# U W1's eight products kept together on TensorE, landmark sums on GpSimd, Newton's first batch ahead of the first weights

## The chip, the core and the metric

The kernel runs on one core of one Trainium2 chip. The metric is the device time of one launch in microseconds. The core has five engines that run side by side, each through its own queue in order: TensorE (matrix products; PE in the rows, its weight loads PEld), VectorE (DVE), ScalarE (ACT), GpSimd (POOL) and SyncE (SP), which here issues the loads.

## What is computed

A Nyström attention with 32 landmarks, then two gated layers of experts without routing. Batch 4, 8 heads, 576 positions, head size 64, so 2304 rows of 512; the hidden size of both layers is 1536. Everything is float32.

```python
q_lm = q.reshape(B, H, m, S // m, D).mean(axis=3)      # m = 32
k_lm = k.reshape(B, H, m, S // m, D).mean(axis=3)
A, Bm, C = sm(q, k_lm), sm(q_lm, k_lm), sm(q_lm, k)    # softmax of scaled products
Z = Bm.T / (norm1(Bm) * norminf(Bm) + 1e-06)
for _ in range(6):
    Z = 2 * Z - Z @ Bm @ Z
x = (A @ Z @ C @ v), rows (b, s), columns (h, d)
x = (silu(x @ w_gate) * (x @ w_val)) @ w_out           # layer 1
x = (sigmoid(x @ w2_gate) * (x @ w2_val)) @ w2_out     # layer 2
```

## The kernel before

The attention's output is never formed. With U = Z C v (32 x 64 per head), layer 1's input product is A (U W1), so the kernel forms U W1 and multiplies it with A. The work is cut into words of a list, each with a batch b, a half g of the heads (four each) or a chunk c of 256 hidden columns:

- F (`front`, lines 111 to 211), for (b, g): the landmark sums of keys and queries (`lm_steps`, `lm`, lines 118 to 122: VectorE adds 18 rows into one, ScalarE copies the result into the second half), their transposition by TensorE (`lt`, line 125), transposition of keys and queries (`tp`), the landmark scores (`cs`, `bm`), exponentials, their transposition (`et`), the products with v (`cv`, scaled into `bc` at line 193), and A's scores (`as`).
- B (`back`, line 231), for b: norms, then Newton's six steps for both halves (`nw` on TensorE, `rw` on VectorE, lines 262 to 284) and the transposition into `UT`. A's normalisation (`a_steps`, line 213) is stepped between Newton's steps.
- U (`uw_steps`, line 413), for (c, b): two PSUM tiles `pu`, one per half, each filled by four products of 64 rows, 32 weight columns and 512 moving columns. Four heads lie in four column strips and the two halves in two row strips of the array, so the eight products use eight different parts of it. Each is two matmul rows in a trace, as the operands are full float32. Afterwards a sum of high and low parts (`split`) goes to SBUF as `uw`.
- G (`gv1_steps`, `pg`, `pv`) and O (`o1_steps`, `po`), for (c, b): the gate and value products with A, and the product with the output weights, 48 matmul rows each.
- I and J: step the weights of a chunk until its input part (four quarters h of `W1`) or its output part is ready. A weight piece is loaded by SP into one of three `raw` buffers and converted by two ScalarE and two VectorE instructions (`convert`, lines 303 to 326), for output weights a split follows.

The order of words up to chunk 1 is written out by hand (line 575); words joined by + are stepped alternately. From chunk 2 on a loop takes U, O of the batch before, and G. Layer 2 follows.

Within that, the tile framework orders each engine's queue: it keeps program order as priority and lets an instruction that is ready by its own estimate go ahead of earlier ones that are not. The order is fixed when the program is built; on the chip each queue is followed strictly. Buffers of a tag (`bufs`) are reused in turn. PSUM tag "o" (two buffers) holds `cs` and `as` of batch 0 and, for c below `OA` = 2, the U and O tiles; from c = 2 on U and O tiles alternate between "o" and "a" (two buffers each). The values `vin` have one buffer, the keys and queries (`in`) four.

Of the kernel before, what the change touches and what calls it, by code (L numbers as in the profile page):

```python
# [9 lines left out]
ALU = mybir.AluOpType  # L10
AX = mybir.AxisListType
# [3 lines left out]
def nystrom_moe_kernel(tc, q, k, v, wg1, wv1, wo1, wg2, wv2, wo2, out):  # L15
    nc = tc.nc
    B, H, S, D = q.shape
    M = 32
    P = 128
# [23 lines left out]
    def ptile(shape, tag, name):  # L43
        return psum.tile(shape, F32, tag=tag, name=name, bufs=PB[tag])
# [4 lines left out]
    ident = cst.tile([P, P], F32, tag="ident", name="ident")  # L49
# [6 lines left out]
    UT = [cst.tile([P, 4, M], F32, tag=f"ut{b}", name=f"ut{b}") for b in range(B)]  # L56
# [4 lines left out]
    def mm(o, l, r, start=True, stop=True):  # L61
        nc.tensor.matmul(o, l, r, start=start, stop=stop, skip_group_check=True)  # L62
# [15 lines left out]
    NU = L // 2  # L78
# [3 lines left out]
    def flat(x):  # L82
        return x.rearrange("p a b -> p (a b)")

    def load_next(b, g, which):
        i = AORDER.index((b, g)) + (1 if which == "v" else 2)
        if i < len(AORDER):
            load_attn(AORDER[i][0], which, AORDER[i][1])
# [12 lines left out]
    def small(tag, shape, nm_, bufs=2):  # L101
        return att.tile(shape, F32, tag=tag, name=f"{tag}{nm_}", bufs=bufs)

    def pst(b, shape, nm, g=0):

        tag = "n" if nm in ("nw", "ut") else "a"
        if b == 0:
            tag = {"tp": "gv", "cs": "o", "as": "o"}.get(nm, tag)
        return ptile(shape, tag, f"{nm}_{b}_{g}")

    def front(b, g):

        nm_ = f"{b}_{g}"

        def sm(tag, shape, bufs=2):
            return small(tag, shape, nm_, bufs)

        def lm_steps(which):
            src = inq[which, b, g]
            lm = sm("lm", [P, 2, D])  # L120
            nc.vector.tensor_reduce(lm[:, 0], src.rearrange("p u d -> p d u"), axis=AX.X, op=ALU.add)  # L121
            nc.scalar.copy(lm[:, 1], lm[:, 0])
            yield
            ps = pst(b, [P, P], "lt", g)
            nc.tensor.transpose(ps, flat(lm), ident)
            bdt = sm("bd" + which, [P, 2, P], 1)
            for w in range(2):
                nc.scalar.activation(bdt[:, w], ps, AF.Copy, scale=pmask[:, w:w + 1])
            yield
            t = sm("kq", [P, NU, P])  # L130
            for i in range(3):
                ps = pst(b, [P, 3, P], "tp", g)
                for j in range(3):
                    u = 3 * i + j
                    nc.tensor.transpose(ps[:, j], flat(src[:, 2 * u:2 * u + 2]), ident)  # L135
                nc.scalar.copy(t[:, 3 * i:3 * i + 3], ps)
                yield
            load_next(b, g, which)
            return bdt, t

        bdk, kT = yield from lm_steps("k")
        bdq, qT = yield from lm_steps("q")
        if g == 0:
            BS[b] = (small("bs", [P, 2, M], b), small("bsm", [P, 2], b), small("bc", [P, 2, 96], b))
        bs, bsm, BC = BS[b]

        cmx = sm("cmx", [P, 2])
        csm = sm("csm", [P, 2])
        nmx = sm("nmx", [P, 1])
        e = sm("e", [P, 3, 2, M, 3], 1)  # L150
        pcs = []
        for w in range(2):
            ps = pst(b, [P, NU, M], "cs", g)
            for h in range(4):
                hs = slice(M * h, M * h + M)
                mm(ps[hs], bdq[:, w, hs], kT[:, :, hs])
            nc.vector.tensor_reduce(cmx[:, w:w + 1], flat(ps), axis=AX.X, op=ALU.max)
            pcs.append(ps)
            yield
        nc.vector.tensor_scalar(nmx, cmx[:, 0:1], cmx[:, 1:2], -1.0, op0=ALU.max, op1=ALU.mult)  # L160
        for w in range(2):
            nc.scalar.activation(e[:, :, w].rearrange("p r t j -> p j r t"),  # L162
                                 pcs[w].rearrange("p (j r) t -> p j r t", r=3), AF.Exp,
                                 bias=nmx, scale=1.0, accum_out=csm[:, w:w + 1])
        yield

        bmx = sm("bmx", [P, 1])
        ps = pst(b, [P, M], "bm", g)
        for h in range(4):
            hs = slice(M * h, M * h + M)  # L170
            mm(ps[hs], bdq[:, 0, hs], bdk[:, 0, hs])
        nc.vector.tensor_reduce(bmx, ps, axis=AX.X, op=ALU.max)
        nc.vector.tensor_scalar(bs[:, g], ps, bmx, None, op0=ALU.subtract)
        nc.scalar.activation(bs[:, g], bs[:, g], AF.Exp, scale=8.0, accum_out=bsm[:, g:g + 1])

        rc = sm("rc", [P, 1])
        nc.vector.tensor_scalar(rc, csm[:, 0:1], csm[:, 1:2], 1e-9, op0=ALU.add, op1=ALU.add)
        nc.vector.reciprocal(rc, rc)
        yield
        eT = sm("eT", [TP, R, P], 1)  # L180
        for hf in range(2):
            ps = pst(b, [TP, 3, P], "et", g)
            for j in range(3):
                r = 3 * hf + j
                nc.tensor.transpose(ps[:, j, :], flat(e[:, r // 2, r % 2]), ident)  # L185
            nc.scalar.copy(eT[:, 3 * hf:3 * hf + 3, :], ps)
            yield
        ps = pst(b, [P, D], "cv", g)
        for r in range(R):
            for h in range(4):  # L190
                mm(ps[32 * h:32 * h + 32, :], eT[:, r, 32 * h:32 * h + 32],
                   inq["v", b, g][:, h, r, :], start=(r == 0), stop=(r == R - 1))
        nc.vector.tensor_scalar(BC[:, g, M:M + D], ps, rc, None, op0=ALU.mult)
        load_next(b, g, "v")
        yield

        s = SX[b, g] = sm("sx", [P, L, M], 3)
        amx = sm("amx", [P, L])
        for i0, i1 in ((0, 5), (5, NU)):
            ps = pst(b, [P, 5, 2 * M], "as", g)  # L200
            for i in range(i0, i1):
                for h in range(4):
                    hs = slice(M * h, M * h + M)
                    mm(ps[hs, i - i0].rearrange("p (w m) -> p w m", w=2), qT[:, i, hs], bdk[:, :, hs])
            x = flat(ps[:, 0:i1 - i0]).rearrange("p (u m) -> p u m", m=M)
            us = slice(2 * i0, 2 * i1)
            nc.vector.tensor_reduce(amx[:, us], x, axis=AX.X, op=ALU.max)
            nc.vector.tensor_tensor(s[:, us], x, amx[:, us, None].to_broadcast([P, 2 * (i1 - i0), M]),
                                    op=ALU.subtract)
            nc.scalar.activation(s[:, us], s[:, us], AF.Exp)  # L210
            yield
# [19 lines left out]
    def back(b):  # L231

        def sm(tag, shape, bufs=2):
            return small(tag, shape, b, bufs)
# [34 lines left out]

        ga = [a_steps(b, g) for g in range(2)]  # L270
        ps = prod(BC)
        RW = sm("rw", [P, 2, 96], 3)
        nc.vector.tensor_tensor(RW, ps, rr[:, :, None].to_broadcast([P, 2, 96]), op=ALU.mult)
        yield
        for it in range(5):
            ps = prod(RW)
            RW2 = sm("rw", [P, 2, 96], 3)
            nc.vector.scalar_tensor_tensor(RW2, RW, 2.0, ps, op0=ALU.mult, op1=ALU.subtract)
            RW = RW2
            step(ga)  # L280
            yield
        ps = prod(RW)
        UU = flat(sm("rw", [P, 2, 96], 3))[:, 0:P].rearrange("p (g d) -> p g d", g=2)
        nc.vector.scalar_tensor_tensor(UU, RW[:, :, M:], 2.0, ps[:, :, M:], op0=ALU.mult, op1=ALU.subtract)
        yield
        ps = pst(b, [P, P], "ut")
        nc.tensor.transpose(ps, flat(UU), ident)
        nc.vector.tensor_copy(flat(UT[b]), ps)
# [10 lines left out]
    W1 = {}  # L299
# [92 lines left out]
    OA = 2  # L392
# [17 lines left out]
    def uw_steps(c, b):  # L410
        pss = [ptile([P, 2 * FC], otag(0, c), f"pu{c}_{b}_{g}") for g in range(2)]

        for g in range(2):
            rows = slice(D * g, D * g + D)
            for h in range(4):
                mm(pss[g][M * h:M * h + M, :], UT[b][rows, h, :], W1[c][rows, h].rearrange("p a b -> p (a b)"))
        for g in range(2):
            w = p1r.tile([P, 2, 2 * FC], F32R, tag="uw", name=f"uw{c}_{b}_{g}", bufs=3)
            UW[c, b, g] = w
            split(w[:, 0, :], w[:, 1, :], pss[g])  # L420
            yield
# [140 lines left out]
    def emit(word, nw=1):  # L562
# [10 lines left out]

    wfill.extend(weights(0, c) for c in range(2))
    first = (
        "I0+F00 F01 B0+F10 U00 F11 J0 B1 G00 I1 F20 U10 J1 O00 G10 O10 U01 G01 F21 U11 "
        "B2+F30 O01 G11 F31 U02 O11 G02 B3 U12 O02 G12 U03 O12 G03 U13 O03 G13"
    )
    for w in first.split():
        emit(w)  # L580
# [77 lines left out]
```

## Time and profile before

| | us |
|---|---|
| median of three runs | 918.42 (917.91 to 919.18) |
| profiled execution | 917.74 |
| its span, first to last instruction | 915.9 |
| TensorE busy in it | 877.8 |
| VectorE busy | 542.2 |
| ScalarE busy | 391.7 |
| GpSimd busy | 0.7 |

A busy TensorE is not TensorE at its peak: matmuls overlap in its pipeline, and a matmul alone counts its whole passage. Two levels of its clock occur: a granted clock of 1.00 is 2.4 GHz, 0.50 is 1.2 GHz, and a value between is a mean over a stretch. The timeline, the table by stretch and the chain of waits (followed back from the end, each step to what released it) are the other views used.

### The profile page before, as it was taken

The numbers are of one execution on the slowest core, as the hardware profiler recorded it, in microseconds if no ns is written. First come the engines' busy times: TensorE is split into PE (matmuls) and PEld (weight loads), VectorE is DVE, ScalarE is ACT, GpSimd is POOL, SyncE is SP. The second block draws the span as 40 slices with busy tenths as digits, with TensorE's granted clock in tenths as the row PEclk, the third lists the DMA queues.
The fourth block names the chain that finished last, engine by engine and source line by source line (L and its number), as shares of the span: only waits on it lengthen the run. The fifth ranks groups of instructions, "written<-read, shape, count | busy, mean of one in ns | idle before, by whom it ended". The sixth has DMA issues, their size and how long they took to land.

```text
span 915.9 us, 16047 instructions
## 1 busy us (share of the span) xinstructions
PE 877.8 (96%) x6588; PEld 741.9 (81%) x6588; DVE 542.2 (59%) x1093; ACT 391.7 (43%) x853; POOL 0.7 (0%) x6
## 2 busy tenths in 40 slices
PE   5499899999999999999999999999999999999997
PEld 4356877778898998998998888888888888888886
DVE  6988857746968678769961154346238236323343
ACT  5568568545725446428652263134116114111111
POOL 0000000000000000000000000000000000000000
PEclk9599999999999999999999999999999999999999
DMA  7666211003513113203110022003004000000132
GB/s 230 222 209 182 70 53 49 7 1 93 155 31 93 47 47 116 69 1 95 46 44 4 0 71 68 1 28 110 0 1 138 1 1 24 1 0 1 47 93 69
DMA packets 27081, 57.66 MB, mean 63 GB/s; under 512 B 4224, under 2 KB 7296, under 8 KB 27008
## 3 DMA queue, kind: packets, MB, share of 16 engines
q1 hardware_dynamic: 25280, 54.28, 19.6%
q10 hardware_dynamic: 1728, 2.36, 1.1%
q8 instruction: 51, 0.84, 0.4%
q14 instruction: 22, 0.18, 0.1%
HBM read 51.90 MB, written 4.72 MB: 62 GB/s over the span
## 4 chain that ended last, share of the span: by engine, by line
PE 88%; DVE 5%; ACT 4%; DMA 1%; issue 1%; SPq 0%; ACTq 0%
PE po L62 33%; PE pg L62 24%; PE pv L62 23%; PE pu L62 3%; PE tp L135 2%; PE nw L62 1%; DMA qin<-in_q_dram 1%; DVE lm L121 1%; PE cs L62 1%; ACT e L162 1%; PE as L62 1%; DVE hl L351 0%; ACT L162 0%; PE et L185 0%; DVE h L441 0%
## 5 line engine op out<-in xcount | busy, mean ns | idle before, releaser
L62 PE MATMUL po<-hh,wo 128*128 128x288 f32 x768 | 162.1, 302 | 1.1 <-DVE uw L351 0.7
L512 DVE TENSOR_TENSOR hf<-hf,pv 128x512 f32<-128x512 f32 (+1 forms) x60 | 38.0, 634 | 193.0 <-PE pv L62 193.0
L62 PE MATMUL po<-wo,h 128*128 128x512 f32 x648 | 152.2, 390 | 0.0
L62 PEld LDWEIGHTS po<-wo,h 128*128 128x128 f32 x648 | 121.1, 188 | 25.4 <-ACT h L350 0.3
L62 PEld LDWEIGHTS po<-hh,wo 128*128 128x128 f32 x768 | 123.0, 188 | 21.1 <-issue 14.4
L62 PE MATMUL pg<-AH,w 128*128 128x512 f32 (+1 forms) x480 | 136.1, 368 | 0.0
L62 PE MATMUL pv<-AH,w 128*128 128x512 f32 (+1 forms) x480 | 136.0, 368 | 0.0
L62 PE MATMUL po<-hl,wo 128*128 128x288 f32 x384 | 114.8, 299 | 0.3 <-DVE hl L351 0.3
L511 ACT ACTIVATE hf<-pg 128x512 f32<-128x512 f32 (+1 forms) x60 | 33.2, 554 | 165.4 <-PE pg L62 158.3
L62 PE MATMUL pg<-AH,uw 128*128 128x288 f32 x576 | 98.7, 298 | 2.3 <-ACT uw L350 1.8
L62 PEld LDWEIGHTS pg<-AH,w 128*128 128x128 f32 x480 | 87.3, 188 | 15.4
L62 PEld LDWEIGHTS pv<-AH,w 128*128 128x128 f32 x480 | 87.1, 189 | 15.0
L62 PE MATMUL pv<-AH,uw 128*128 128x288 f32 x576 | 96.7, 296 | 1.2 <-ACT sg L439 1.2
L62 PEld LDWEIGHTS pg<-AH,uw 128*128 128x128 f32 x576 | 83.1, 188 | 8.4 <-ACT uw L350 4.9
L350 ACT CAST h<-hf 128x512 fp32r<-128x512 f32 (+1 forms) x60 | 34.6, 576 | 123.2 <-DVE hf L512 123.2
L533 DVE TENSOR_TENSOR oacc<-po,oacc 128x512 f32<-128x512 f32 x90 | 61.9, 691 | 41.1 <-PE po L62 39.9
L62 PEld LDWEIGHTS pv<-AH,uw 128*128 128x128 f32 x576 | 82.9, 188 | 3.2 <-ACT sg L439 2.2
L62 PE MATMUL pg<-x1l,w 128*128 128x512 f32 x192 | 74.7, 389 | 0.0
L62 PE MATMUL pv<-x1l,w 128*128 128x512 f32 x192 | 74.7, 389 | 0.0
L62 PEld LDWEIGHTS po<-hl,wo 128*128 128x128 f32 x384 | 72.3, 188 | 2.4 <-issue 0.9
L467 DVE TENSOR_TENSOR acc<-po,acc 128x288 f32<-128x288 f32 x128 | 56.0, 452 | 18.2 <-PE po L62 17.5
L439 ACT ACTIVATE sg<-pg 128x288 f32<-128x288 f32 x96 | 39.2, 409 | 51.7 <-PE pg L62 51.1
(113 smaller groups left out, 1062.8 us busy)
## 6 DMA issues: line engine op xcount, KB each, us to landing
raw<-in_moe_w_out_dram SPq DMA_DIRECT2D x24, 512.0 KB, 4.2
raw<-in_moe_w_gate_dram SPq DMA_DIRECT2D x48, 128.0 KB, 3.3
raw<-in_moe_w_val_dram SPq DMA_DIRECT2D x48, 128.0 KB, 3.1
raw<-in_moe_w_gate_dram SPq DMA_DIRECT2D x24, 256.0 KB, 2.9
raw<-in_moe_w_val_dram SPq DMA_DIRECT2D x24, 256.0 KB, 3.3
kin<-in_k_dram SPq DMA_DIRECT2D x8, 576.0 KB, 3.9
qin<-in_q_dram SPq DMA_DIRECT2D x8, 576.0 KB, 5.7
vin<-in_v_dram SPq DMA_DIRECT2D x8, 576.0 KB, 4.9
```

The lines of the kernel that those rows point to most:

```text
L62: nc.tensor.matmul(o, l, r, start=start, stop=stop, skip_group_check=True)
L121: nc.vector.tensor_reduce(lm[:, 0], src.rearrange("p u d -> p d u"), axis=AX.X, op=ALU.add)
L135: nc.tensor.transpose(ps[:, j], flat(src[:, 2 * u:2 * u + 2]), ident)
L162: nc.scalar.activation(e[:, :, w].rearrange("p r t j -> p j r t"), pcs[w].rearrange("p (j r) t -> p j r t", r=3), AF.Exp, bias=nmx, scale= ...
L350: nc.scalar.copy(hi, x)
L439: nc.scalar.activation(sg, pss[0], AF.Silu)
L467: nc.vector.tensor_tensor(sl, ps, sl, op=ALU.add)
L511: nc.scalar.activation(h, pss[0], AF.Sigmoid)
L512: nc.vector.tensor_tensor(h, h, pss[1], op=ALU.mult)
L533: nc.vector.tensor_tensor(acc, ps, acc, op=ALU.add)
```

## The change

Four edits. In `uw_steps` the eight products are emitted half by half within a head, from the last quarter h = 3 to the first, at the highest priority, and in a region that keeps TensorE's instructions in emission order; for c below 2 a product of the identity with two of its own columns into the first tile goes ahead. In `lm_steps`, for all (b, g) but (0, 0), GpSimd adds the 18 rows by halving (9 + 9, then 4 + 4, 2 + 2, the odd row, and the last pair twice, once into each half of `lm`) in place of VectorE's sum and ScalarE's copy; `lm` gets one buffer in place of two, and a new `ls` tile has one. Newton's `rw` tiles get two buffers in place of three. And the list of words has F00, F01 and B0 ahead of I0, and another order up to F20.

```diff
         def lm_steps(which):
             src = inq[which, b, g]
-            lm = sm("lm", [P, 2, D])
-            nc.vector.tensor_reduce(lm[:, 0], src.rearrange("p u d -> p d u"), axis=AX.X, op=ALU.add)
-            nc.scalar.copy(lm[:, 1], lm[:, 0])
+            lm = sm("lm", [P, 2, D], 1)
+
+            if (b, g) > (0, 0):
+                x = sm("ls", [P, NU, D], 1)
+                nc.gpsimd.tensor_tensor(x, src[:, 0:NU], src[:, NU:], op=ALU.add)
+                nc.gpsimd.tensor_tensor(x[:, 0:4], x[:, 0:4], x[:, 4:8], op=ALU.add)
+                nc.gpsimd.tensor_tensor(x[:, 0:2], x[:, 0:2], x[:, 2:4], op=ALU.add)
+                nc.gpsimd.tensor_tensor(x[:, 0], x[:, 0], x[:, 8], op=ALU.add)
+                for w in range(2):
+                    nc.gpsimd.tensor_tensor(lm[:, w], x[:, 0], x[:, 1], op=ALU.add)
+            else:
+                nc.vector.tensor_reduce(lm[:, 0], src.rearrange("p u d -> p d u"), axis=AX.X, op=ALU.add)
+                nc.scalar.copy(lm[:, 1], lm[:, 0])
...
-        RW = sm("rw", [P, 2, 96], 3)
+        RW = sm("rw", [P, 2, 96], 2)
...
-            RW2 = sm("rw", [P, 2, 96], 3)
+            RW2 = sm("rw", [P, 2, 96], 2)
...
-        UU = flat(sm("rw", [P, 2, 96], 3))[:, 0:P].rearrange("p (g d) -> p g d", g=2)
+        UU = flat(sm("rw", [P, 2, 96], 2))[:, 0:P].rearrange("p (g d) -> p g d", g=2)
...
-        for g in range(2):
-            rows = slice(D * g, D * g + D)
-            for h in range(4):
-                mm(pss[g][M * h:M * h + M, :], UT[b][rows, h, :], W1[c][rows, h].rearrange("p a b -> p (a b)"))
+        with tc.high_priority(), tc.manual_schedule(engines={mybir.EngineType.PE}):
+            if c < OA:
+
+                mm(pss[0][:, 0:2], ident, ident[:, 0:2])
+            for h in range(3, -1, -1):
+                for g in range(1, -1, -1):
+                    rows = slice(D * g, D * g + D)
+                    mm(pss[g][M * h:M * h + M, :], UT[b][rows, h, :], W1[c][rows, h].rearrange("p a b -> p (a b)"))
...
-        "I0+F00 F01 B0+F10 U00 F11 J0 B1 G00 I1 F20 U10 J1 O00 G10 O10 U01 G01 F21 U11 "
-        "B2+F30 O01 G11 F31 U02 O11 G02 B3 U12 O02 G12 U03 O12 G03 U13 O03 G13"
+        "F00 F01 B0 I0 F10 U00 G00 J0 F11 I1 U10 B1 O00 G10 J1 F20 O10 U01 G01 "
+        "F21 U11 B2+F30 O01 G11 F31 U02 O11 G02 B3 U12 O02 G12 U03 O12 G03 U13 O03 G13"
```

## Rows read from the trace of the kernel before

**Rows 1.** The page's 40 slices: TensorE's busy tenths, its granted clock in tenths

```profile
PE   5499899999999999999999999999999999999997
...
PEclk9599999999999999999999999999999999999999
```

**Rows 2.** Stretches: length, busy us (count) PE PEld DVE ACT POOL, PEclk, DMA, GB/s

```profile
14.50:31.50 17.00, 10.31 (x239) 7.55 (x239) 13.81 (x43) 15.39 (x43) 0.00 (x0) 0.79 0.75 232
31.50:43.40 11.90, 3.02 (x66) 1.96 (x67) 11.90 (x22) 5.46 (x12) 0.00 (x0) 0.50 0.68 207
43.40:56.30 12.90, 11.54 (x171) 6.95 (x171) 10.05 (x21) 6.19 (x20) 0.00 (x0) 0.81 0.53 162
56.30:75.60 19.30, 18.78 (x230) 11.82 (x224) 17.25 (x33) 17.10 (x36) 0.00 (x0) 1.00 0.73 223
75.60:115.10 39.50, 35.22 (x557) 29.48 (x554) 33.61 (x78) 25.81 (x68) 0.00 (x0) 1.00 0.36 105
115.10:159.20 44.10, 43.76 (x627) 32.62 (x627) 29.04 (x71) 31.57 (x74) 0.00 (x0) 1.00 0.17 45
```

**Rows 3.** Timeline, SP's issues, then TensorE, idle time and releaser in brackets

```profile
21.25 3.39 SPq L346 DMA_DIRECT2D raw<-in_moe_w_out_dram  x2
...
29.63 0.53 SPq L71 DMA_DIRECT2D vin<-in_v_dram  x1
...
35.52 1.51 PE L62 MATMUL cv<-vin,eT 96*32 96x64 f32 x48 [3.46 <-DMA vin<-in_v_dram]
...
42.84 0.55 PE L62 MATMUL nw<-bc 32*32 32x96 f32 x8 [5.40 <-DVE bc L193]
```

**Rows 4.** Timeline, VectorE, 42 to 46 us

```profile
42.52 0.27 DVE L193 TENSOR_SCALAR bc<-cv,rc 128x64 f32<-128x64 f32 x1
...
43.72 2.10 DVE L121 TENSOR_REDUCE lm<-kin 128x64 f32<-128x1152 f32 x1
...
45.75 0.34 DVE L278 SCALAR_TENSOR_TENSOR rw<-rw,nw 128x192 f32<-128x192 f32 x1
```

**Rows 5.** Chain of waits, 56 to 280 us: start, length, what, count

```profile
63.92 0.20 PE lt L125
...
65.24 0.97 PE pu L62 x2
...
96.72 2.23 DVE lm L121
...
102.70 2.13 DVE lm L121
...
263.23 1.02 PE pu L62 x16
```

**Rows 6.** Timeline, TensorE: start, duration, engine, line, operation, tiles, shapes, count; U groups

```profile
56.30 1.04 PE L62 MATMUL pu<-w,ut 64*32 64x512 f32 x2
...
72.32 1.69 PE L62 MATMUL pu<-w,ut 64*32 64x512 f32 x8
...
74.59 1.05 PE L62 MATMUL pu<-w,ut 64*32 64x512 f32 x6
...
115.11 1.68 PE L62 MATMUL pu<-w,ut 64*32 64x512 f32 x16
...
203.43 1.09 PE L62 MATMUL pu<-w,ut 64*32 64x512 f32 x16
...
234.36 1.08 PE L62 MATMUL pu<-w,ut 64*32 64x512 f32 x14
```

**Rows 7.** Lines 121, 122: engine, operation, count: duration ns min/median/max, starts, shapes

```profile
L121 DVE TENSOR_REDUCE lm<-kin x8: 2078/2141/2211, 4.6 to 142.3; 128x64 f32<-128x1152 f32 x8
...
L122 ACT COPY lm<-lm x16: 240/244/258, 6.7 to 148.9; 128x64 f32<-128x64 f32 x16
```

**Rows 8.** Groups by line, VectorE, 14.5 to 115.1: busy us, mean ns, idle

```profile
L319 DVE SCALAR_TENSOR_TENSOR cv<-cv,cv 128x512 uint32<-128x512 uint32 x14 | 9.6, 683 | 4.0 <-ACT cv L317 4.0
```

**Rows 9.** Timeline, GpSimd, its last row

```profile
1.01 0.29 POOL masks.py:199 TENSOR_SCALAR_AFFINE_SELECT ident<-ident 128x128 f32<-128x128 f32 x1
```

## The prediction

> **What bounds the kernel now.** I read the page first, for which engine is full and where. TensorE is at 9 tenths from the fourth slice to the end and ahead of that at 4 to 8 tenths with a granted clock of 5 and 9 tenths in slices two and three [rows 1]. So the run has a start of some 75 us that is not TensorE's, and a long rest that is. The table by stretch says whose the start is [rows 2]: from 31.5 to 43.4 us VectorE is busy for all 11.90 us, TensorE for 3.02 with its clock at half (1.2 GHz), ScalarE for 5.46. From 14.5 to 75.6 VectorE works 13.81 + 11.90 + 10.05 + 17.25 = 53.0 of 61.1 us (87%), ScalarE 44.1. After 115 us TensorE is busy 43.76 of 44.10. What holds TensorE in the start is seen in the timeline: the value products `cv` of group (0,1) wait until 35.52 for `vin`, whose load SP issued at 29.63, behind weights [rows 3]; then Newton's first product stands at 42.84 after 5.40 us of waiting for `bc` [rows 3], which VectorE gets to only at 42.52 [rows 4], since its queue has landmark sums, attention normalisation and conversions ahead of it. Inside Newton the step at 45.75 comes straight after a sum that began at 43.72 and took 2.10 [rows 4].
>
> Then the U products. One group is eight products, 16 matmul rows in the trace. Where all 16 stand together they take 1.02 us on the chain [rows 5]; a run of two, that is one product alone, takes 0.97 [rows 5], and a run of 14 seen by its own duration takes 1.08 against 1.09 for 16 [rows 6]. The price is per run, whatever its length. Seven of the 24 groups come in more than one run, the first begins at 56.30, the last run of the last at 234.36 [rows 6]; after that all are whole.
>
> **U products together.** Extra runs, each at the 0.97 of a lone product: U00, U02 and U20 one each; U11 and U12 two each (a lone product, four, three); U10 a lone product, then a run of 1.69 that is two runs overlapped, then one more: 0.97 + 1.69 + 0.97 - 1.02 = 2.6; U01 two half groups without other work between, 1.68 against 1.09, so 0.59 [rows 5, 6]. In all 0.97 x 3 + 1.9 x 2 + 2.6 + 0.59 = 9.9 us of TensorE. U00 and U10 (3.6) lie in the start, where TensorE is not the bound, and I count nothing for them; the other 6.3 us lie where it is busy 35.2 of 39.5 and 43.8 of 44.1 us [rows 2], and I count them whole. The new order takes the last W1 quarter (h = 3) first, so the eight wait for it together; the waiting costs nothing as before they could not finish earlier either, and queued behind the first product on TensorE are only its own seven. For c < 2 a product of two columns with the identity is added, eight in all. No row shows it. From below it is 0: it stands where TensorE waits for the PSUM buffer anyway. From above it is two passes like the identity transposition `lt`, 0.20 us each on the chain [rows 5], so 0.4. I take 0.2, as it has a full-width weight load like `lt` but hardly any columns; six of them after the start make +1.2 (0 to 2.4). Together -5.1 (-6.3 to -3.9). The 16 groups of c >= 2 are whole now and stay so: only their order turns.
>
> **Landmark sums to GpSimd, Newton ahead of the weights.** Of 16 sums of 2.14 us on VectorE [rows 7] 14 go, with 14 ScalarE copies behind them. Eight of these (F01 two ahead of 14.5, F10, F11, F20 two each) are done before U10 ends at 75.6 [rows 6]. VectorE's work from 14.5 to 75.6 becomes 53.0 - 6 x 2.14 = 40.2 us; at the same 87% that is 46 us, a gain of 15. ScalarE's 44.1 us at 87% needs 50.7, a gain of 10.4 [rows 2]. The second is the tighter one and I take it: -10.4. The lower end of the gain is 0, if the late `vin` stays where it is. That it moves: B0 and with it F01's end now stand ahead of I0, so in SP's order the load of `vin` (0,1) and the next keys and queries no longer stand behind the fourth W1 quarter and two `raw` loads of the output weights, issued from 21.25 for 3.39 us [rows 3]. They are queued after it, and the first conversions with them (ScalarE and VectorE two instructions each per quarter). That costs nothing as long as the gaps in the two queues before U00 take 4 x 2 x 0.683 = 5.5 us of VectorE [rows 8]; if they don't, U00 waits that long, still less than what Newton gains. G00, ahead of J0 and F11, fills TensorE while F11 is prepared. What is late next is ScalarE's conversions for c = 1, which is why I go by its bound. In the rest two sums stand on the chain itself, 2.23 at 96.72 and 2.13 at 102.70 [rows 5]; they vanish, but their neighbours in VectorE's queue take part of the place: -2 (0 to -4.4).
>
> GpSimd's price: a sum is six additions over 576 + 256 + 128 + 3 x 64 = 1152 columns. GpSimd's only row that reads data takes 0.29 us for 128 columns [rows 9]; by it 9 x 0.29 = 2.6 us, and 5.3 if two inputs cost double. Against 2.14 + 0.24 [rows 7] that is 0.3 to 2.9 us more latency per sum. It is hidden: nothing else is in GpSimd's queue, the keys and queries of (1,0) on are loaded ahead of use, and F01's values, which need the one `vin` buffer that F00 must first set free, land behind its keys and queries by far. The single `lm` and `ls` buffers make the query sum wait for the key sum's transposition, behind which only GpSimd's own additions queue. Two `rw` buffers do: a step's output goes where the step before the last was already read.
>
> Here is what speaks against this part. No row shows VectorE and GpSimd working side by side; GpSimd's last row ends at 1.30 us [rows 9]. The Trainium skill (SBUF — State Buffer, "Who interferes with whom") says that a VectorE instruction with two SBUF inputs and a GpSimd instruction that reads SBUF exclude each other for the whole instruction. The Trainium skill (GPSIMD Engine Reference, section 3.1) has 4497 ns for an addition over 2048 columns, which makes an estimate of 2.5 us a sum; by it the sum of my terms stays as it is, and by the exclusion it is the third rival.
>
> **The sum.** The profiled execution took 917.74 us (span 915.9): 917.74 - 10.4 - 5.1 - 2.0 = 900.2. The median of the runs is 0.7 above it: 901. Own range: 918.4 - 15 - 6.3 - 4.4 = 893 to 918.4 - 3.9 - 3.5 (a third of the start's gain) = 911.
>
> **Rivals.** (1) The start doesn't shorten: conversions, deferred, hold U00 and U10 as VectorE did. For it: ScalarE is busy 17.10 of 19.30 us from 56.3 to 75.6, and 15.39 of 17 from 14.5 [rows 2]. Against it: 5.46 and 6.19 of 11.9 and 12.9 between. Then only packing and the two sums count: 918.4 - 5.1 - 2 = 911. (2) The change doesn't keep the products together, because the second PSUM buffer comes free later than the first, as in U01's halves [rows 6]. Then 918.4 - 10.4 - 2 = 906, and 14 us more (24 x 0.59) in the extreme case that every group halves. (3) Slower: GpSimd's sums hold VectorE. The place is VectorE's queue from 14.5 to 115 us; of the conversions' two instructions with two SBUF inputs the first alone is 14 x 0.683 = 9.6 us [rows 8], both some 19 of 86.6 us there. If a sum holds VectorE for as long as it lasts, the price per sum is 2.6 - 2.14 = +0.5 us; 14 make +7, less 5.1: 920. From (5.1 / 14) + 2.14 = 2.5 us of hold per sum on it is slower; at 4 us it is 939. Against it: only part of VectorE's instructions have two SBUF inputs, so hold for the full time should be rare. (4) Nothing measurable: the start's gain is given back between 75 and 159 us by waits that TensorE, idle there for 4.6 us only [rows 2], doesn't have now.
>
> **How the numbers follow.** Forecast 0.58, rival 1 0.17, rival 2 0.08, rival 3 0.12, rival 4 0.05. 0.2% (1.8 us) is about what a measurement of this kernel tells from no change. Faster: the forecast, rival 1 and most of rival 2: 0.81; same (rival 4 and a little of 2) 0.06; slower (rival 3 and the far end of 2) 0.13. The range takes in the forecast's own bounds, rival 1 with its start a little later still, and rival 2: 892 to 917.
>
> **What would show it.** In the new profile: runs of 16 `pu` rows in all 24 groups, at about 1.0 us; `vin` (0,1) issued well before 29.63 and Newton's first product some 10 us ahead of 42.84; U10's last product at about 65 instead of 75.6; VectorE short of 9 tenths in slices two to five; GpSimd rows of 2.6 to 5.3 us per sum. Wrong would be: VectorE's two-input rows grown longer than 0.683 beside GpSimd's (rival 3), `vin` still late (rival 1), or TensorE waiting before `pg` for W1.

## The result and the profile after

The changed kernel takes 908.27 us (median of 4 runs, 907.62 to 909.72), the kernel before 918.8 (917.91 to 920.79): a ratio of 0.9879, 95% interval 0.986 to 0.9898. That is 10.5 us of gain by the medians (11.1 by the ratio), inside the forecast range of 892 to 917, and 7 us short of the 901 forecast. The profiled execution took 907.64 us (span 905.9) against 917.74 (915.9).

The page of the changed kernel, its span, its busy times and 40 slices:

```profile
span 905.9 us, 16181 instructions
...
PE 872.2 (96%) x6604; PEld 744.0 (82%) x6604; DVE 523.4 (58%) x1079; ACT 396.3 (44%) x845; POOL 55.8 (6%) x90
...
PE   5778999999999999999999999999999999999997
...
DVE  4977665765977678769861153355347236433342
ACT  5688477755653355537643262143125114111111
POOL 4530323000000000000000000000000000000000
PEclk9898999999999999999999999999999999999999
```

TensorE's second slice rose from 4 to 7 tenths and its clock there from 5 to 8; but the third and fourth fell from 9 and 9 to 7 and 8 [rows 1]. The page also gives the reading that I use for every kernel below: span = TensorE busy + TensorE idle. Before it was 915.9 = 877.8 + 38.1; now it is 905.9 = 872.2 + 33.7. So 5.6 us of work went away and 4.4 us of idling.

The same stretches as [rows 2], with the same columns:

```profile
14.50:31.50 17.00, 12.29 (x316) 8.60 (x314) 13.44 (x37) 11.57 (x36) 12.90 (x21) 1.00 0.90 237
31.50:43.40 11.90, 8.81 (x122) 4.91 (x122) 11.42 (x24) 8.32 (x17) 5.75 (x8) 0.71 0.47 143
43.40:56.30 12.90, 10.27 (x187) 7.76 (x186) 10.97 (x25) 11.02 (x23) 2.24 (x3) 1.00 0.72 213
56.30:75.60 19.30, 13.40 (x108) 8.62 (x108) 13.51 (x28) 16.18 (x37) 6.75 (x10) 0.75 0.66 211
75.60:115.10 39.50, 37.02 (x551) 30.20 (x551) 28.46 (x74) 24.50 (x58) 11.33 (x18) 0.99 0.42 110
115.10:159.20 44.10, 42.74 (x631) 33.04 (x632) 25.85 (x71) 32.67 (x72) 12.21 (x21) 1.00 0.19 54
```

From 31.5 to 43.4 us TensorE now works 8.81 us instead of 3.02. But from 56.3 to 75.6 it works 13.40 instead of 18.78, at 0.75 of its clock instead of 1.00: the hole has moved behind U00.

The timeline of SP, and then of TensorE (start, duration, operation, count, idle time and releaser in brackets), where the prediction had named its milestones:

```profile
17.39 0.34 SPq L71 DMA_DIRECT2D vin<-in_v_dram  x1
```

```profile
27.54 0.37 PE L62 MATMUL nw<-bc 32*32 32x96 f32 x8 [1.09 <-DVE bc L203]
...
44.62 1.09 PE L62 MATMUL pu<-w,ut 64*32 64x512 f32 x16 [1.08 <-DVE w L333]
...
70.25 1.96 PE L62 MATMUL pu<-w,ut 64*32 64x512 f32 x16 [3.52 <-DVE w L333]
...
110.69 0.38 PE L62 MATMUL pu<-ident 128*128 128x2 f32 x2
...
111.82 1.09 PE L62 MATMUL pu<-w,ut 64*32 64x512 f32 x16
```

`vin` (0,1) is issued at 17.39 (29.63 before) and Newton's first product stands at 27.54 (42.84) [rows 3]. U00 ends at 45.71 against 60.12, 14.4 us earlier. U10 ends at 72.21 against 75.65: of the 14.4 us 3.4 are left. All 24 groups are now single runs of 16 rows [rows 6]: 1.09 us, and 1.96 at the low clock.

### The profile page after: what moved, and what is told of

Read it like the earlier page. It is cut to its first block, busy times and chain, and to the rows that moved or that the text cites. A ratio compares the mean times of both kernels' runs of the same rounds, so it can differ in the third digit from the quotient of the medians.

```text
span 905.9 us, 16181 instructions
## 1 busy us (share of the span) xinstructions
PE 872.2 (96%) x6604; PEld 744.0 (82%) x6604; DVE 523.4 (58%) x1079; ACT 396.3 (44%) x845; POOL 55.8 (6%) x90
## 4 chain that ended last, share of the span: by engine, by line
PE 89%; DVE 4%; ACT 4%; issue 1%; DMA 1%; SPq 0%; ACTq 0%; DVEq 0%
PE po L62 33%; PE pv L62 24%; PE pg L62 24%; PE pu L62 3%; PE tp L145 1%; PE nw L62 1%; PE cs L62 1%; ACT L453 1%; DMA raw<-in_moe_w_val_dram 1%; PE as L62 1%; PE cv L62 1%; DVE lm L131 0%; DMA kin<-in_k_dram 0%; ACT e L172 0%; PE et L195 0%
## 5 line engine op out<-in xcount | busy, mean ns | idle before, releaser
L62 PE MATMUL po<-hh,wo 128*128 128x288 f32 x768 | 164.9, 303 | 1.4 <-ACT acc L479 0.9
L526 DVE TENSOR_TENSOR hf<-hf,pv 128x512 f32<-128x512 f32 (+1 forms) x60 | 38.1, 634 | 194.2 <-PE pv L62 194.2
L62 PEld LDWEIGHTS po<-hh,wo 128*128 128x128 f32 x768 | 124.4, 188 | 17.1 <-issue 12.9
L360 ACT CAST h<-hf 128x512 fp32r<-128x512 f32 (+1 forms) x60 | 34.6, 576 | 124.2 <-DVE hf L526 124.2
L481 DVE TENSOR_TENSOR acc<-po,acc 128x288 f32<-128x288 f32 x128 | 56.4, 454 | 16.1 <-PE po L62 15.6
L324 ACT ACTIVATE cv<-raw 128x512 f32<-128x512 f32 x72 | 48.5, 674 | 26.5 <-DVE cv L333 11.3
```

Source lines behind the costliest of these rows:

```text
L324: nc.scalar.activation(t0, hiw.bitcast(F32), AF.Copy, scale=2.0 ** -112)
L360: nc.scalar.copy(hi, x)
L481: nc.vector.tensor_tensor(sl, ps, sl, op=ALU.add)
L526: nc.vector.tensor_tensor(h, h, pss[1], op=ALU.mult)
```

## The experiments

Three edits are in the change: the emission list ("list"), the eight products kept together ("together"), the sums on GpSimd ("sums"; the buffer counts of `lm`, `ls` and `rw` go with them). I ran every combination, the eight corners, then took single causes apart. Each kernel is told as an edit to the kernel before or to the changed one. The corners, with the page's TensorE figures of the profiled execution (idle is span minus busy); the column of us is the ratio times 918.4:

| list | together | sums | ratio to before, 95% interval | us | TensorE busy + idle |
|---|---|---|---|---|---|
| - | - | - | 1 | 0 | 877.8 + 38.1 |
| yes | - | - | 0.9993 [0.9979, 1.0007] | -0.6 | 882.2 + 34.2 |
| - | yes | - | 0.9965 [0.9954, 0.9976] | -3.2 | 871.4 + 43.2 |
| - | - | yes | 1.002 [1.001, 1.0031] | +1.8 | 881.5 + 36.7 |
| yes | - | yes | 0.9967 [0.9952, 0.9983] | -3.0 | 882.2 + 30.4 |
| yes | yes | - | 0.995 [0.9934, 0.9966] | -4.6 | 879.0 + 34.6 |
| - | yes | yes | 0.9956 [0.9941, 0.9972] | -4.0 | 875.1 + 37.3 |
| yes | yes | yes | 0.9879 [0.986, 0.9898] | -11.1 | 872.2 + 33.7 |

A busy microsecond at the low clock does less: U10's 16 rows above take 1.96 us there and 1.09 at the high one. Of the busy column, the part that lies at a granted clock of 0.50 in the first 160 us is, in the table's order, 11.9, 16.9, 12.4, 12.8, 11.9, 32.7, 23.3 and 15.6 us. So the corners differ in the clock too, not only in their work.

**The list alone** (order_only): the kernel before with the new list.

```
-        "I0+F00 F01 B0+F10 U00 F11 J0 B1 G00 I1 F20 U10 J1 O00 G10 O10 U01 G01 F21 U11 "
+        "F00 F01 B0 I0 F10 U00 G00 J0 F11 I1 U10 B1 O00 G10 J1 F20 O10 U01 G01 "
...
```

> The kernel before with the new list of words alone. Theory A (the list sets the start: the values of (0,1) are loaded ahead of the weights): Newton's first product some 10 us ahead of 42.84, U00's last product before 52, and the total 4 to 7 us under before. Theory B (VectorE's sums set the start): the values come early but VectorE still has F01's and F10's sums, 4 x 2.14 = 8.6 us, in the same stretch, so U00 gains at most 6 us and the total lies within 2 us of before.

918.08 us, as theory B had it. `vin` (0,1) is issued at 18.74 and U00 ends at 54.19 (60.12 before), but U10 ends at 77.57 (75.65). What the start gains is gone again by U10, and TensorE's work grows by 4.4 us. Of that 4.1 us are in the U products' own rows (40.73 us against 36.67): they still come in 10 extra runs (9 before), and the runs have moved into the low clock, where U00's first product takes 1.91 us instead of 1.04.

**Together alone** (together_only): the kernel before with the new loops.

```
-        for g in range(2):
...
-            for h in range(4):
...
+        with tc.high_priority(), tc.manual_schedule(engines={mybir.EngineType.PE}):
+            if c < OA:
+                mm(pss[0][:, 0:2], ident, ident[:, 0:2])
+            for h in range(3, -1, -1):
+                for g in range(1, -1, -1):
...
```

> The kernel before with the new emission of the U products alone (dummy product included). The prediction's term: 5.1 us under before (6.3 to 3.9), 24 groups in one run of 16 rows each at 1.09 us. Rival (the freed TensorE time goes into waits for VectorE and ScalarE that now stand bare): 0 to 2 us under before, with TensorE's idle time between 75 and 235 us grown by what its busy time lost.

915.76 us. All 24 groups are whole and 6.4 us of TensorE's work is gone, but TensorE idles 5.1 us more: U01 ends at 123.25 (116.79 before), since the eight wait for the last quarter where single products used to fill in.

**Sums alone** (sums_only): the kernel before with the new `lm_steps`.

```
+            if (b, g) > (0, 0):
+                x = sm("ls", [P, NU, D], 1)
+                nc.gpsimd.tensor_tensor(x, src[:, 0:NU], src[:, NU:], op=ALU.add)
...
```

> The kernel before with 14 landmark sums on GpSimd alone (and the buffer counts of ls, lm and rw that go with them). Theory (VectorE is relieved of 2.14 us a sum and held for about 0.6): Newton's steps no longer wait behind sums, U00 2 to 5 us earlier, total 3 to 5 us under before. Rival (the exclusion between GpSimd and VectorE takes the relief back): total within 1 us of before or above it.

920.55 us: slower by 0.1 to 0.3%. With the old list `vin` (0,1) is late as before, and Newton's first product waits for it longer than before (44.95 against 42.84). In its timeline of TensorE:

```profile
44.95 0.54 PE L62 MATMUL nw<-bc 32*32 32x96 f32 x8 [7.63 <-DVE bc L203]
```

VectorE's instructions that lie beside GpSimd's came out 10.9 us longer in all than the same ones before. TensorE idles 1.4 us less than before but works 3.7 more, and the U products come in 12 extra runs (9 before).

**All but together** (not_together): the changed kernel with the old loops.

> The changed kernel with the old emission of the U products, so new list and GpSimd sums alone. If the parts add up as predicted: 908.3 + 5.1 = 913.4, with split groups back in the trace. If keeping the products together is worth nothing in this order, or costs (it makes U10's first product wait for the last W1 quarter, and the dummy holds a PSUM buffer early): 907 to 909.

915.17 us, above both expectations. Its U10, in the timeline of TensorE:

```profile
55.89 1.05 PE L62 MATMUL pu<-w,ut 64*32 64x512 f32 x4 [0.55 <-DVE w L333]
...
66.14 1.77 PE L62 MATMUL pu<-w,ut 64*32 64x512 f32 x4 [1.12 <-DVE w L333]
...
70.21 3.22 PE L62 MATMUL pu<-w,ut 64*32 64x512 f32 x8 [1.18 <-DVE w L333]
```

Six groups are split again, with 11 extra runs. Against the changed kernel TensorE works 10.0 us more and idles 3.3 less. 11 runs at the 0.97 of [rows 5] are 10.7 us. That the two agree so well is in part chance: the U products' own rows differ by 14.6 us (41.7 against 27.0 without the identity products), since U10's later runs stand at the low clock (1.77 and 3.22 us above), and other work goes the other way.

**All but sums** (sums_on_vector): the changed kernel with the old `lm_steps`.

> The changed kernel with all landmark sums back on VectorE, so new list and kept-together products. Theory (the list needs VectorE's relief, each alone having given nothing): U00's last product near 54, as with the list alone, and the total 914 to 917, the list's 0 and the products' 2.5 added. Rival (GpSimd's sums only cost, by holding VectorE's instructions by 9 us in all): 908 or less.

914.45 us; U00 ends at 50.69 and U10 at 77.23, 5.0 us later each than in the changed kernel. With the other two edits in place the sums on GpSimd are worth 6.5 us (0.995 to 0.9879); on the kernel before they cost 1.8. The clock has a large part in the 6.5 us. The stretches up to 160 us in which the granted clock is 0.50, added up (length, then busy us of each engine), in this kernel:

```profile
sum 37.54, PE 32.70 PEld 21.86 DVE 30.45 ACT 22.81 POOL 0.00; mean PE 5.45 PEld 3.64 DVE 5.08 ACT 3.80 POOL 0.00
```

and in the changed one:

```profile
sum 17.07, PE 15.62 PEld 9.91 DVE 12.61 ACT 13.91 POOL 5.34; mean PE 5.21 PEld 3.30 DVE 4.20 ACT 4.64 POOL 1.78
```

By the 1.96 to 1.09 of U10's rows, 17.1 us more of TensorE's work at the low level cost some 7.6 us, an estimate; its busy time is 6.8 us longer (879.0 against 872.2).

**All but the list** (no_order): the changed kernel with the old list.

> The changed kernel with the emission list of the kernel before (weights first, Newton's second half behind the fourth W1 quarter); the sums on GpSimd and the eight products together stay. The missing corner of the three edits. Theory: the sums and the packing are of use only where the start is free to move up, so without the new list what is left is what each brought alone on the kernel before, -3.2 us for the packing and +1.9 for the sums: 916.5 to 918.5 us, vin (0,1) issued near 29.6 again and U00's products ending near 58 to 60. Rival: the sums and the packing help each other without the list (VectorE's freed time serves the conversions for U01 to U12): 910 to 913 us, and then the list is worth only some 4 us. In the rival the gain shows between 75 and 235 us, in the theory nowhere before 235.

914.32 us, between the two expectations. U00 ends at 55.86, U10 at 77.51, U01 at 121.55 (116.79 before). The seventh O begins at 214.2 us in the changed kernel and at 220.9 here. The list is worth 7.1 us where the other two are in. The table's last line is more than the sum of its single edits (-2.0). My reading is that each frees something that the others use. No run excludes another reading: the framework orders the queues anew for every kernel, and a part of each corner may be the order that it came to.

**The sum's work doubled** (double_sums): the changed kernel, with two more additions over 576 columns in each sum.

```
                 nc.gpsimd.tensor_tensor(x, src[:, 0:NU], src[:, NU:], op=ALU.add)
+                nc.gpsimd.tensor_tensor(x, src[:, 0:NU], src[:, NU:], op=ALU.add)
+                nc.gpsimd.tensor_tensor(x, src[:, 0:NU], src[:, NU:], op=ALU.add)
```

> The changed kernel with two more additions of 128x576 on GpSimd behind each sum, whose result nobody reads: 14 x 2 x 1.41 = 39 us more of GpSimd reading SBUF. In the changed kernel VectorE's instructions beside GpSimd's are 8.8 us longer in all, some 0.16 us per us of GpSimd. If this hold is on the path: 6 us more of it, total 2 to 5 us above the changed kernel's 908.3. If GpSimd's queue and VectorE's slack absorb it (GpSimd waits 89 us for TensorE's transposition as it is): 908 to 909.5.

926.49 us, 1.009 [1.007, 1.011] of the kernel before, 18 us above the changed one and far above both expectations. GpSimd's busy time grows from 55.8 to 99.9 us, and VectorE's lengthening from 8.8 us in 20 instructions to 23.5 in 36. Its waits (engine, tile, line, what it waited for: us, times, longest):

```profile
PE nw L62 <- DVE rw L290: 7.4, 6, 3.2
...
PE lt L137 <- POOL lm L129: 5.5, 2, 2.7
```

Both costs show: the hold of VectorE inside Newton, and TensorE waiting for the sums. How the 18 us divide between them stays open.

**No identity product, halves 0 then 1** (no_dummy): the changed kernel, high priority and the manual schedule kept.

```
-            if c < OA:
-                mm(pss[0][:, 0:2], ident, ident[:, 0:2])
...
-                for g in range(1, -1, -1):
+                for g in range(2):
```

> The changed kernel without the identity product, with the halves in the order 0, 1 inside each head (so that the first tile is still written first). By the rows the identity product takes 0.31 to 0.38 us on TensorE's chain; eight make 2.7: total 905.5 to 907. If its purpose is to take the first tile's wait away from the eight, groups break into halves as U01 did before, 0.59 each for up to eight groups: 909 to 912. If both cancel or it hides in waits: 908.

930.56 us, 1.013 [1.0115, 1.0145], above all three expectations. 22 of the 24 groups split, also all 16 of c >= 2, which have no identity product in either kernel. The timeline of TensorE at one of these:

```profile
404.69 1.04 PE L62 MATMUL pu<-w,ut 64*32 64x512 f32 x2
405.67 0.40 PE L62 MATMUL po<-hh,wo 128*128 128x288 f32 x1
...
406.66 1.08 PE L62 MATMUL pu<-w,ut 64*32 64x512 f32 x14
```

One product goes, then other work, then the other seven. TensorE's work grows by 21.9 us; 22 lone products at 0.97 make 21.3. So for c >= 2, where the turn of the halves is the only edit, it is their order that keeps the eight together. My reading of why: with half 0 first the second product needs half 1's PSUM buffer, which comes free later, and with half 1 first the first product already needs it. For c < 2 the two edits weren't taken apart.

**Key and query loads off SP** (keys_on_act): in the changed kernel's chain of waits the last W1 quarter of U10 goes back to a load:

```profile
62.69 0.33 SPq L75
...
63.07 2.92 DMA raw<-in_moe_w_val_dram
...
67.54 0.66 ACT cv L324
...
68.78 0.70 DVE cv L329
...
69.51 0.70 DVE w L333
...
70.25 1.96 PE pu L62 x16
```

The `raw` load at 63.07 stands behind a key load (L75, 62.69) that waited for its buffer. The edit sends the key and query loads of b > 1 through ScalarE's queue.

```
-            nc.sync.dma_start(t, src[b, 4 * g:4 * g + 4].rearrange("h (t u) d -> (h t) u d", u=L))
+            (nc.scalar if b > 1 else nc.sync).dma_start(t, src[b, 4 * g:4 * g + 4].rearrange("h (t u) d -> (h t) u d", u=L))
```

> The changed kernel with the key and query loads of batches 2 and 3 issued from ScalarE's queue in place of SP's, so that the last quarter of W1 for chunk 1 doesn't stand in SP's queue behind the keys of (2,1), which wait there for a buffer until 62.69. Theory (this queue gives back the start's gain): that load is issued near 59.2, U10's products stand near 66 in place of 70.25, and the total is 2 to 4 us under 908.3. Rival (ScalarE, busy 16.2 of 19.3 us there, sets U10): U10 within 1 us of 70, total 907.5 to 909.

907.83 us, 0.9887 [0.987, 0.9903]; U10 ends at 74.78, 2.6 us later than in the changed kernel. The load is gone from in front and U10 comes no earlier: SP's queue is not what gave the gain back. U01 and U11, though, end 5.5 and 5.9 us earlier (at 107.36 and 111.45), and the time is the same all the same: these milestones don't measure what the start is worth.

**U10 ahead of F11** (u10_first): the changed kernel with U10 and its weights emitted ahead of the front of group (1,1).

```
-        "F00 F01 B0 I0 F10 U00 G00 J0 F11 I1 U10 B1 O00 G10 J1 F20 O10 U01 G01 "
+        "F00 F01 B0 I0 F10 U00 G00 J0 I1 U10 F11 B1 O00 G10 J1 F20 O10 U01 G01 "
```

> The changed kernel with U10, and the weights that it needs, emitted ahead of the front of group (1,1): J0 I1 U10 F11 in place of J0 F11 I1 U10. U10's products ended at 72.21 in the changed kernel, only 3.4 us ahead of before. Theory: the last W1 quarter of c=1 stands behind the softmax of F11 in ScalarE's and VectorE's queues (ScalarE 16.2 of 19.3 us, part of it the wait for nmx), an order and not an amount of work; with the weights ahead U10's products end at 64 to 68, G10 follows, and the time falls by 2 to 6 us, to 902 to 906. Rival: what bounds the start is the amount of work of ScalarE and VectorE up to U01, whatever the order; then U10 comes earlier but F11's values and with them B1, U01 and U11 come as much later, and the time is 907 to 910. Third: F11's later end holds TensorE more than before, 911 to 914.

904.76 us, 0.9861 [0.984, 0.9883], the lowest median of all kernels here; the intervals of this one and the changed kernel (0.986 to 0.9898) overlap. The expected time came, the expected place did not: U10 ends at 71.46, only 0.75 us earlier, but TensorE is busy 54.37 us up to 75.6 (51.72 in the changed kernel), and U01 ends at 110.27 instead of 112.91. F11's products now stand beside O00's, which start at 73.5 instead of 75.5.

**ScalarE relieved at VectorE's cost** (kq_on_vector): the changed kernel with the copies of the transposed keys and queries on VectorE.

```
-                nc.scalar.copy(t[:, 3 * i:3 * i + 3], ps)
+                if (b, g) > (0, 0):
+                    nc.vector.tensor_copy(t[:, 3 * i:3 * i + 3], ps)
...
```

> The changed kernel with the copies of the transposed keys and queries (three of 128x384 for each, 0.49 us on ScalarE) made by VectorE for all groups but (0,0): some 42 instructions, 20 us of ScalarE's work moved to VectorE. If ScalarE's amount of work bounds the start (16.2 of 19.3 us ahead of U10), U10's products end 2 to 3 us ahead of 72.2 and the time is 904 to 906. If the two engines' queues bound it together, or GpSimd's sums hold the moved copies as they hold other VectorE instructions (8.8 us over 20 instructions so far), U10 stays at 71 to 74 and the time is 907 to 911.

914.74 us, 0.9966 [0.9954, 0.9978]: worse than both expectations. U10 ends at 76.62. The stretch up to there, columns as in the table by stretch:

```profile
14.50:76.62 62.12, 45.11 (x710) 28.84 (x712) 52.83 (x126) 42.32 (x94) 25.50 (x40) 0.79 0.68 199
```

VectorE is back at 52.83 of 62.12 us (85%), what it was before the change: the list and the sums had made room on it that isn't there to give away.

**ScalarE loaded** (twice_copied): the changed kernel with ScalarE's six copies of group (1,1) made twice.

```
                 nc.scalar.copy(t[:, 3 * i:3 * i + 3], ps)
+                if (b, g) == (1, 1):
+                    nc.scalar.copy(t[:, 3 * i:3 * i + 3], ps)
```

> The changed kernel with ScalarE's six copies of the transposed keys and queries of group (1,1) made twice, to the same place: six more copies, some 0.37 to 0.49 us each, 2.2 to 2.9 us of work that goes to ScalarE alone and stands between U00 and U10, where ScalarE is busy 23.43 of 26.50 us in the changed kernel. Theory: ScalarE's amount of work sets U10 there; then U10's products end 2 to 3 us later, at 74 to 75.2, and the time is 909.5 to 911. Rival: U10 is set by a chain of waits across ScalarE, VectorE, TensorE and SP's transfers, with ScalarE's 3 us of idle time to take the copies in; then U10 ends less than 1 us later, 72 to 73, and the time is 907 to 909.

909.23 us, 0.9907 [0.9883, 0.9931], not to be told from the changed kernel. In its timeline of TensorE, U10 and U01:

```profile
72.95 1.96 PE L62 MATMUL pu<-w,ut 64*32 64x512 f32 x16 [2.01 <-DVE w L335]
...
111.84 1.09 PE L62 MATMUL pu<-w,ut 64*32 64x512 f32 x16
```

U10 ends at 74.91, 2.7 us later, as ScalarE's amount of work would have it. But the framework also put conversions of U10's weights behind the new copies in ScalarE's queue, so that amount and order are not parted here, and keys_on_act moved U10 by 2.6 us with no work added. And U01 ends at 112.93 against 112.91: U10's end, which the theory, like my prediction, took as the measure of the start, doesn't move U01.

## Why the prediction was right and where it was not

**The start, -10.4.** This term was mis-sized. The moves came as forecast: `vin` at 17.39, Newton 15 us ahead where some 10 were named, U00 14.4 earlier. Then I gave U10 a gain by dividing ScalarE's 44.1 us by 87%, which was VectorE's rate in a stretch that VectorE bounded. The stretches up to U00's end and on to U10's end, before:

```profile
14.50:75.65 61.15, 43.71 (x698) 28.33 (x699) 53.01 (x117) 44.17 (x108) 0.00 (x0) 0.80 0.69 210
60.12:75.65 15.53, 15.10 (x113) 10.06 (x113) 14.67 (x28) 15.26 (x33) 0.00 (x0) 1.00 0.82 253
...
14.50:60.12 45.62, 28.61 (x587) 18.27 (x587) 38.33 (x90) 28.91 (x75) 0.00 (x0) 0.74 0.64 195
```

and after:

```profile
14.50:72.21 57.71, 41.38 (x694) 27.36 (x696) 46.51 (x104) 44.38 (x104) 27.64 (x40) 0.89 0.71 209
45.71:72.21 26.50, 19.05 (x241) 13.67 (x244) 19.38 (x41) 23.43 (x51) 8.99 (x12) 0.89 0.71 222
...
14.50:45.71 31.21, 22.33 (x454) 13.69 (x452) 27.13 (x64) 20.95 (x54) 18.65 (x28) 0.89 0.71 197
```

ScalarE's column (the fourth pair) is the point. Its work ahead of U10 is 44.17 us before and 44.38 after: the forecast's 44.1 held. But only 20.95 of it lies ahead of U00 now (28.91 before), at 67% of the time, and 23.43 instead of 15.26 come behind it, at 88%. The list pushes weights' work from the one side of U00 to the other. By stretch that is 31.2 + 23.4 / 0.88 = 57.8 us against 61.15, the 3.4 that U10 got; as the 88% is read from the same stretch, this says where the gain went and does not prove why. twice_copied fits ScalarE as what holds U10 there, since 2.2 to 2.9 us of copies moved it by 2.7, but amount and order are not parted in it. So rival 1's reason ("conversions, deferred, hold U00 and U10") is borne out for U10 and was wrong for U00.

The prediction also misread [rows 1]: TensorE stands at 9 tenths from the third slice, not the fourth, and is busy for 18.78 of 19.30 us from 56.3 to 75.6 at the full clock [rows 2]. By the rule used for the stretches behind it, where TensorE counts as full at 35.2 of 39.5 us, the last 19 us of the "start of some 75 us that is not TensorE's" were TensorE's as well.

And U10 was the wrong milestone. TensorE's idle time fell by 4.4 us in the whole run, where start and sums together had been given 12.4; u10_first took another 4.2 off it (33.7 to 29.5) with U10 nearly where it was, twice_copied put U10 back by 2.7 at nearly the same span (906.1), and keys_on_act moved U10 back and U01 forward at the same span (905.9). My reading is that it counts how much other work TensorE has while a front is being prepared; u10_first fits that, and no run shows it by itself.

**VectorE's 40.2 us.** Measured 46.51. The difference is the hold: in this stretch 13 of VectorE's instructions, each overlapped by one of GpSimd's, are 5.9 us longer than the same ones before; 40.2 + 5.9 = 46.1. So VectorE, forecast short of 9 tenths in slices two to five, still stands at 9 in slice two. VectorE's timeline after (start, duration):

```profile
23.58 1.25 DVE L248 TENSOR_SCALAR bsm<-bsm 128x2 f32<-128x2 f32 x1
...
29.20 1.32 DVE L267 TENSOR_SCALAR rr<-rr 128x2 f32<-128x2 f32 x1
...
34.16 1.13 DVE L227 TENSOR_SCALAR asm<-asm 128x18 f32<-128x18 f32 x1
```

before:

```profile
37.86 0.15 DVE L257 TENSOR_SCALAR rr<-rr 128x2 f32<-128x2 f32 x1
...
38.60 0.15 DVE L217 TENSOR_SCALAR asm<-asm 128x18 f32<-128x18 f32 x1
```

and GpSimd's timeline after:

```profile
14.11 1.41 POOL L124 TENSOR_TENSOR ls<-qin 128x576 f32<-128x576 f32 x1
15.60 0.73 POOL L125 TENSOR_TENSOR ls<-ls 128x256 f32<-128x256 f32 x1
16.40 0.46 POOL L126 TENSOR_TENSOR ls<-ls 128x128 f32<-128x128 f32 x1
16.94 0.32 POOL L127 TENSOR_TENSOR ls<-ls 128x64 f32<-128x64 f32 x1
18.41 0.60 POOL L129 TENSOR_TENSOR lm<-ls 128x64 f32<-128x64 f32 x2 [1.16 <-PE lt L135]
...
22.99 1.80 POOL L124 TENSOR_TENSOR ls<-qin 128x576 f32<-128x576 f32 x1
...
29.08 1.41 POOL L124 TENSOR_TENSOR ls<-kin 128x576 f32<-128x576 f32 x1
...
33.85 1.40 POOL L124 TENSOR_TENSOR ls<-qin 128x576 f32<-128x576 f32 x1
```

Each of the three slow VectorE rows begins inside or just behind the start of a 576-column addition of GpSimd's and ends with it (24.8, 30.5, 35.3); two work on two columns. GpSimd's addition is held too at 22.99: 1.80 instead of 1.41. This is rival 3's mechanism. In the whole run it is 8.8 us over 14 sums, 0.63 per sum, a quarter of the 2.5 from which I had it decide. That it decides beyond some point double_sums shows: at 1.7 us per sum, and sums some 2.8 us longer, the kernel is slower than before, by both costs together.

What I had wrong is which instructions are held: I counted those with two SBUF inputs, and the three above have one. Of the 13 instructions six have one input and take 4.0 of the 5.9 us; the sign that I named, the conversions' two-input rows of 0.683, grew by 0.44 us at most. The Trainium skill (SBUF — State Buffer, "Who interferes with whom") names copies and `tensor_scalar` instructions too, when they run in a mode that uses both ports; I had drawn only on its sentence about two inputs. The rows agree with the wider one, as far as they go: none shows the mode.

**GpSimd's price, 2.6 to 5.3 us.** 1.41 + 0.73 + 0.46 + 0.32 + 0.60 = 3.52 us, inside; the estimate of 2.5 us was too low. It was hidden, as forecast: in the changed kernel no wait of TensorE's for it is among the larger ones, and GpSimd itself waits 89.1 us in all for `lt` to free its one `lm` buffer. The sums are worth 6.5 us with the other two edits and less than nothing on the kernel before, so the step "two sums on the chain, -2" measured neither. That it depends on whether `vin` has come is my reading: without the list, but with the products kept together, the sums bring 0.8 us.

**Together, -5.1.** The price per run came out near: 11 extra runs against none are 10.0 us of TensorE's work (all but together against the changed kernel), and 0.97 each makes 10.7, with the clock's part as said there. "The waiting costs nothing" was wrong: TensorE idles 3.3 us more there, 5.1 on the kernel before. Net it is 6.7 us of span in its place (8.1 by the ratios) and 1.3 alone (3.2 by the ratios). That this lies around the 5.1 forecast is partly luck: 1.9 us of it come in each case from the groups of c >= 2, which the forecast put at nothing (see below). Up to the 13th O the edit brings 4.7 us in its place, and alone it loses 0.8. The identity products take 0.28 to 0.38 us from start to end, but TensorE's next row begins 0.13 to 0.24 us behind their start, nearer to the 0.2 taken than to the upper bound.

"The 16 groups of c >= 2 are whole and stay so: only their order turns" came true, but no_dummy shows that the turn is what holds them under the new scheduling. Rival 2 had the mechanism (the second buffer comes free later), and its price for a split was too small: some 1.0 each, 22 us in all, not 0.59.

**Not in my sum.** From the 13th O on, where TensorE is full, the changed kernel gains 1.9 us more (8.1 us ahead at the 13th O, 10.0 at the last). In the kernel before, the groups by line from 235.5 to 470 us name waits there (last columns: idle before, and releaser):

```profile
L62 PE MATMUL po<-hh,wo 128*128 128x288 f32 x528 | 108.7, 300 | 0.9 <-DVE uw L351 0.7
L62 PE MATMUL po<-hl,wo 128*128 128x288 f32 x264 | 78.3, 297 | 0.3 <-DVE hl L351 0.3
```

In the changed kernel there is none in this stretch. The corners say which edit brings the 1.9 us. From the start of the 13th O to that of the 24th TensorE has the same 1240 rows in all eight; they take 160.4 to 160.5 us in the four kernels with the old loops and 158.5 in the four with the new ones, whatever the list and the sums. So it belongs to "together", at groups that were whole before: 0.8 us is idling of the kind above, and for the other 1.1 I have no name. In no_dummy, where the ten groups of this stretch are split, it takes 171.5 us.

**In sum**: the forecast of faster, its range and the milestones up to U00 held; a range of 892 to 917 takes in nearly any gain, so that alone says little. By place the 7 us that lack are the start's: 10.4 claimed at U10 and 3.4 come, while behind U10 6.6 come of 7.1 (8.1 us ahead at the 13th O, 10.0 at the last). By edit the forecast was further off: list and sums bring 3.0 us where 12.4 stood in the sum, and keeping the products together adds 8.1 to that where 5.1 stood. That terms add up was taken for granted, and they don't. Open are how the 18 us of double_sums divide, and how much of each corner is the clock's and the queues' order.

## What to carry to other kernels

Bound each stretch by the engine that fills that stretch: work moved across a milestone doesn't vanish, it fills the next stretch, and a rate read on one engine is no rate of another. Split the span into busy and idle time of the engine that bounds the kernel, for every variant: it showed here at once that keeping products together buys work and pays in idling, and that there is less of that idling with the list and the freed VectorE; read the busy time with its granted clock beside it. Edits that bring 2 us in all one by one can bring 11 together, so each is tried in the presence of the others. Where products must stand together in a queue, let the first of them need the resource that comes last.

## What was not expected of the hardware

- A VectorE instruction on two columns took 1.25 and 1.32 us beside a GpSimd addition, and 0.15 to 0.17 without one.
- A product that stands alone costs as much as eight (0.97 against 1.02 us): 22 lone products added 21.9 us of TensorE's work, 1.00 each.
- The clock's low level came back in the changed kernel: from 56.3 to 75.6 us, where TensorE has work for 13.40 of 19.30 us, it is granted 0.75, and U10's 16 rows take 1.96 us there instead of 1.09. Before, with work for 18.78 us, it was granted 1.00.
